# A fused attention and feed-forward kernel: weight splitting spread over six slots, and a tensor operand for a small addition

## Chip, cores, metric

One core of a Trainium2 chip. The metric is the device time of one execution in microseconds (us), the median of several runs; lower is better.

## The reference

```python
def _attn_ref(q, k, v, w1, b1, w2):            # B 4, heads 8, S 576, D 64
    scores = scale * np.matmul(q, k.transpose(0, 1, 3, 2))
    bias = np.maximum(x @ w1 + b1, 0.0) @ w2    # x from positions alone
    scores = scores + bias.transpose(2, 0, 1)[None, :, :, :]
    attn = np.exp(scores - np.max(scores, axis=-1, keepdims=True))
    attn = attn / (np.sum(attn, axis=-1, keepdims=True) + 1e-09)
    return np.matmul(attn, v)
...
x = attn_out.transpose(0, 2, 1, 3).reshape(B * S, H * D)          # 2304 x 512
h = x @ w_in;  x = (h * np.clip(h + 3.0, 0.0, 6.0) / 6.0) @ w_out   # 512 -> 2048 -> 512
x = (sigmoid(x @ w_gate) * (x @ w_val)) @ w_out2                    # 512 -> 1536 -> 512
```

## The kernel before

**Stages.** First the position bias is computed and sent to DRAM (about 0 to 58 us of the span). Then comes the attention (about 57 to 340 us), then the first feed-forward layer (to about 741 us), then the gated one.

**Attention.** The work is 16 attention units n, each two heads of one batch entry; a unit has nine steps s (NSTEP), so there are 144 steps t. The loop at the end of the attention code goes over slots i of two steps each (slot_of_two, L463), so one unit takes four and a half slots and two units take nine. In a slot stand the scores of its two steps (L342, TensorE) with the bias added and the row extreme taken on VectorE (L346), the products with V of an earlier unit (L432, L435, result scaled at L444), the exponentials on ScalarE (L362), and the transposes of the slot before (L400, L408, L415), whose results VectorE and ScalarE copy out of PSUM (L392, L390). After steps 5 and 8 of a unit, invert (L365) adds 1e-9 to the row sums (L368), takes the reciprocal (L369) and spreads it out (L373); turn_inv transposes that one slot later (L379). prep (L304) splits Q and K of the next unit into a high and a low part; its work on GpSimd is at L314 and L318.

**Weights.** The feed-forward weights are split into a high and a low part too. A weight unit is one 128x512 block of 8-byte integers. The Loader makes it in these operations: a DMA of 512 KB into one of two raw buffers (L159), the absolute value of the upper word on ScalarE (L175), a lower bound (the max) on VectorE (L176), a shift on VectorE (L184), two merges with the raw words on VectorE (L186, L188), then the high part on ScalarE and the low part on GpSimd (L192, L193). The first ten units stay in SBUF slots of their own. Before the change, Loader.whole emits a whole unit at once, at slots i = 12, 18, 24, ..., 66 (EVERY is 6). The next units come from Loader.tick, called at slots 70 and 73 (PRIME) and right behind the attention.

**What sets the order.** The program is emitted in the order described, and that order is the priority. A scheduler then lays out each engine's queue at compile time: where its model has an engine free and an operation of lower priority ready, that operation goes ahead. So an operation can stand in its engine's queue earlier than its slot. The DMA of each of the ten units is tied (issue_after) behind the latest load of V on SyncE's queue (L295), which is emitted at step 0 of each attention unit; the other operations of a weight unit are tied to nothing but their data and buffers. Each engine runs its queue in order.

Of the kernel before, what the change touches and what calls it, by code (L numbers as in the profile page):

```python
# [10 lines left out]
F32 = mybir.dt.float32  # L11
F32R = mybir.dt.float32r
I32 = mybir.dt.int32
AF = mybir.ActivationFunctionType
ALU = mybir.AluOpType
# [3 lines left out]
P = 128  # L19
# [6 lines left out]
NSTEP = 9  # L26
# [18 lines left out]


NPRE = 10
EVERY = 6
PRIME = (NU * NSTEP // 2 - 2, NU * NSTEP // 2 + 1)
NALL = 19  # L50

# [45 lines left out]
def block_kernel(ctx: ExitStack, tc: tile.TileContext, q, k, v, mlp, w_in, w_out, w_gate, w_val, w_out2, dist_d,  # L97
                 rows_d, out):
    nc = tc.nc
    pool = lambda **kw: ctx.enter_context(tc.tile_pool(**kw))  # L100
    keep = pool(name="keep", bufs=1)
# [6 lines left out]
    tok = lambda t: [xj[t // 2][:, c, TW * (t % 2) : TW * (t % 2) + TW] for c in range(4)]  # L108
    half = keep.tile([P, 1], F32, name="half")
    one = keep.tile([P, 1], F32, name="one")  # L110
    slots = [keep.tile([P, 2, 512], F32R, name=f"slot{i}") for i in range(NPRE)]
    nbias = [dram.tile([16 * (8 * RK - 1) * (min(P, S - P * c) // 16) + 16], F32, name=f"nbias{c}") for c in range(5)]
    part_d = [dram.tile([P, 4, TW], F32, name=f"part{t}") for t in range(NTILE)]
# [10 lines left out]
    def ring(name):  # L124

        if name == "z":
            return stg.tile([P, 512], F32, name="z", bufs=3)
        return stg.tile([P, 2, 512], F32, name="raw", bufs=2)

    class Loader:  # L130
# [31 lines left out]
        def magnitude(self, i):  # L162
            if i in self.raw:
# [11 lines left out]
                nc.scalar.activation(z, raw[..., 1].bitcast(F32), AF.Abs)  # L175
                nc.vector.tensor_scalar(out=z, in0=z, scalar1=2.0**-15, scalar2=None, op0=ALU.max)  # L176

        def assemble(self, i):
            if i not in self.raw:
                return  # L180
            self.raw.pop(i)
            z, raw = self.z[i]
            zi = z.bitcast(I32)
            nc.vector.tensor_scalar(out=zi, in0=zi, scalar1=3, scalar2=0x3FFFFFF8, op0=ALU.logical_shift_left,  # L184
                                    op1=ALU.bitwise_and)
            nc.vector.scalar_tensor_tensor(out=zi, in0=raw[..., 1], scalar=-0x40000000, in1=zi,  # L186
                                           op0=ALU.bitwise_and, op1=ALU.bitwise_or)
            nc.vector.scalar_tensor_tensor(out=zi, in0=raw[..., 0], scalar=29, in1=zi,  # L188
                                           op0=ALU.logical_shift_right, op1=ALU.bitwise_or)

        def halve(self, z, slot, eng):
            nc.scalar.copy(slot[:, 0], z)  # L192
# [5 lines left out]
        def stage(self, z, idx):  # L198
            hl = self.pair()
            self.halve(z, hl, nc.gpsimd)  # L200
            nc.sync.dma_start(w_d[idx], hl.bitcast(F32))
            self.staged.add(idx)
# [23 lines left out]
                self.mix(to[1], to[2])  # L226
            self.done = i + 1

        def whole(self):
            i = self.n  # L230
            for stage in (self.dma, self.magnitude, self.assemble):
                stage(i)
            self.finish(i, nc.gpsimd)
            self.n += 1

        def tick(self):
            i = self.n
# [24 lines left out]
    load = Loader()  # L262
# [102 lines left out]
    def invert(n, c0, c1):  # L365

        r = sums[n % 3][:, 2 * c0 : min(2 * c1, NSTEP)]
        nc.vector.tensor_scalar(out=r, in0=r, scalar1=1e-9, scalar2=None, op0=ALU.add)  # L368
        nc.vector.reciprocal(r, r)  # L369
        for s0, s1, w in ((0, 6, 64),) if c1 == 3 else ((6, 8, 64), (8, 9, P)):  # L370
            o = spread[:, 64 * s0 : 64 * s0 + (s1 - s0) * w].rearrange("p (s w) -> p s w", w=w)
            i = sums[n % 3][:, s0:s1].unsqueeze(2).to_broadcast(o.shape)
            nc.scalar.copy(o, i)  # L373
# [75 lines left out]
    last_v = [None]  # L449
# [3 lines left out]
    for n in range(NU):  # L453
        i = (NSTEP * n + 5) // 2 + 2
# [8 lines left out]
    def slot_of_two(i):  # L463

        for t in steps(i):
            scores(t)
            n, s = seq[t]
            p, b = divmod(n, B)
            if s == 0:
                last_v[0] = load_v(n)  # L470
            if b == B - 1 and p + 1 < NPAIR and (s % 2 == 1 or s == 8):
                load_bias(p + 1, s // 2)
        for n, a, g in AV.get(i, ()):
            av(n, a, g)
            if g == 4:
                av_out(n, a)
        for t in steps(i):
            expo(t)
        for t in steps(i - 1):
            n, s = seq[t]  # L480
            if s in (5, 8):
                invert(n, s // 6 * 3, s // 6 * 2 + 3)
        for t in steps(i - 2):
            n, s = seq[t]
            if s in (5, 8):
                turn_inv(n, s // 6 * 3, s // 6 * 2 + 3)
        for t in steps(i - 1):
            n, s = seq[t]
            with tc.issue_after(last_s[0].ins):
                trans(t)  # L490
                if s in REM:
                    trans_rem(n, REM[s])
        for t in steps(i):
            if t in PREP:
                n, h = PREP[t]
                prep(n, h)
            for k, (n, h) in PREP.items():
                if h == 1 and n + 1 < NU and t == k + 3:
                    load_qk(n + 1)
# [6 lines left out]
    with ExitStack():  # L506
# [9 lines left out]
        nc.vector.memset(warm, 0.0)  # L516
        nc.vector.memset(half, 0.5)
        nc.vector.memset(one, 1.0)
        nc.scalar.activation(low[0][:, 0:1], one, AF.Relu)
        bias_ps = ExitStack()  # L520
        bp = bias_ps.enter_context(tc.tile_pool(name="bp", bufs=4, space=PSUM))
# [5 lines left out]
        for i in range(2):  # L527
# [5 lines left out]
                                op1=ALU.mult)  # L533
# [30 lines left out]
        for G in range(NG):  # L564
            hid = [hids[(4 * G + ct) % 12] for ct in range(4)]
            nd = max(S - 16 * G, 16 * G + 16)
            for ct in range(4):
# [3 lines left out]
                else:  # L571
                    nc.vector.tensor_scalar(out=hid[ct][:, 0:nd], in0=tbl[:, 0:nd], scalar1=bpsi[:, 1, qd : qd + 1],  # L572
                                            scalar2=None, op0=ALU.max)
# [23 lines left out]
        def split_x(t, cs=range(4)):  # L597
            for c in cs:
                XH, XL = XS[t % 2][:, 0, c], XS[t % 2][:, 1, c]
                nc.scalar.copy(XH, tok(t)[c])  # L600
                eng = nc.gpsimd if 1 in XS else nc.vector
                eng.tensor_tensor(out=XL, in0=tok(t)[c], in1=XH.bitcast(F32), op=ALU.subtract)

        def project(t, slot, ps=None):
            XH, XL = XS[t % 2][:, 0], XS[t % 2][:, 1]
            ps = mp.tile([P, 512], F32, name="h", bufs=4) if ps is None else ps
            for c in range(4):
                wh = slot[:, 0, P * c : P * c + P]
                wl = slot[:, 1, P * c : P * c + P]
                nc.tensor.matmul(ps[:, 0:TW], wh, XH[:, c], start=(c == 0), stop=False)  # L610
                nc.tensor.matmul(ps[:, 0:TW], wl, XH[:, c], start=False, stop=False)  # L611
                nc.tensor.matmul(ps[:, 0:TW], wh, XL[:, c], start=False, stop=(c == 3))  # L612
            return ps[:, 0:TW]

        def hardswish(g, ph):
            nc.scalar.activation(g, ph, AF.Relu, bias=half, scale=1.0 / 6.0)  # L616
            nc.vector.scalar_tensor_tensor(out=g, in0=g, scalar=1.0, in1=ph, op0=ALU.min, op1=ALU.mult)  # L617
            return g
# [5 lines left out]
        for i in range(NSLOT):  # L624
            slot_of_two(i)
            if i == NS // 2:
                w = keep.tile([P, 8 * TW], F32R, name="early")
                XS[0] = w.rearrange("p (r c t) -> p r c t", r=2, c=4)
                split_x(0)
            if i in (NS // 2 + 1, NS // 2 + 2):  # L630
                f = len(begun)
                begun[f] = hardswish(ring("z")[:, 0:TW], project(0, slots[2 * f], pp.tile([P, 2, 512], F32, name="s")[:, 0]))
            if i % EVERY == 0 and i > 10 and load.n < NPRE:
                with tc.issue_after(last_v[0].ins):
                    load.whole()
            if i in PRIME:
                load.tick()

# [185 lines left out]
        def gate_val(base, G, whole):  # L824
            sig, late = {}, {}

            def gate(i, u, ps):
                s = sig[i] = half_t("s", 6)
                if u is None:
                    nc.scalar.activation(s, ps, AF.Sigmoid)  # L830
                else:
                    add(s, u, ps)
                    nc.scalar.activation(s, s, AF.Sigmoid)

            def val(i, u, ps):
                v = ps
                if u is not None:
                    v = half_t("v", 3)
                    add(v, u, ps)
                s = sig[i]  # L840
                last_g[0] = nc.vector.tensor_tensor(out=s, in0=s, in1=v, op=ALU.mult)
                last_h[0] = nc.scalar.copy(G[:, i, 0], s)  # L842
                nc.gpsimd.tensor_tensor(out=G[:, i, 1], in0=s, in1=G[:, i, 0].bitcast(F32), op=ALU.subtract)  # L843

            a, b = Products(base, 0, gate), Products(base, 1, val)
            for p, ks in ((a, range(7)), (b, range(7))) if whole else ((a, range(4)), (b, range(4)), (a, range(4, 7)),
                                                                      (b, range(4, 7))):
                p.run(ks)
# [77 lines left out]
```

## Time and profile before

| what | us |
|---|---|
| median of 3 runs | 1158.08 |
| lowest, highest | 1157.95, 1161.23 |
| the profiled execution | 1160.52 |
| its span | 1158.7 |

TensorE is PE in the profile (PEld is its weight load), VectorE is DVE, ScalarE is ACT, GpSimd is POOL and SyncE is SP. In a timeline row the columns are the start in us from the span's start, the length in us, the engine, the line of the code, the operation, the tiles written and read, and the number of instructions merged into the row. The bracket at the end is idle time of the engine just before, and what ended it. Ends of matmuls are modelled, so distances between starts tell more of PE than its busy time does.

### The profile page before, as it was taken

The page shows a single profiled execution, that of the slowest core. Times are in us where ns is not written, and L with a number is a line of the kernel's source. Part 1 is how long each engine was busy: PE and PEld are TensorE (multiplying, and loading weights), DVE is VectorE, ACT ScalarE, POOL GpSimd, SP SyncE. Part 2 cuts the span into 40 slices and gives each one's busy share as a digit, 9 for nine tenths or more (in the row PEclk, how much of TensorE's full clock was granted, in tenths as well). Part 3 has the DMA queues.
Part 4 walks back from the last instruction along what each step waited for, and adds up shares of the span by engine and source line. Part 5 has one row for each costly group of instructions (what it writes and reads, how often), then busy time and mean ns, then how long its engine had stood idle before and what let it go on. Part 6 is the DMA issues. An engine that isn't in the chain of part 4 may idle for free.

```text
span 1158.7 us, 19146 instructions
## 1 busy us (share of the span) xinstructions
PE 1135.9 (98%) x6862; PEld 1012.2 (87%) x6862; DVE 772.8 (67%) x1495; ACT 588.4 (51%) x1296; POOL 422.6 (36%) x342
## 2 busy tenths in 40 slices
PE   8799999999999999999999999999999999999998
PEld 3277777777779999999999999999899898998997
DVE  8977878788868887355386775585367655644443
ACT  7988887877855545454455454342333222221221
POOL 0154544544316433232347445261333223311211
PEclk9999999999999999999999999999999999999999
DMA  6854436353213665249467759976878848757532
GB/s 203 298 162 110 158 95 183 112 165 103 78 55 110 209 218 200 101 174 340 167 228 255 253 189 357 395 261 251 308 254 309 311 165 299 285 181 258 191 109 73
DMA packets 83183, 236.82 MB, mean 204 GB/s; under 512 B 9616, under 2 KB 12304, under 8 KB 83088
## 3 DMA queue, kind: packets, MB, share of 16 engines
q1 hardware_dynamic: 83088, 235.60, 58.6%
q8 instruction: 54, 0.88, 0.3%
q14 instruction: 41, 0.34, 0.1%
HBM read 154.15 MB, written 81.41 MB: 203 GB/s over the span
## 4 chain that ended last, share of the span: by engine, by line
PE 84%; DVE 6%; ACT 2%; DMA 2%; issue 1%; POOL 1%; SPq 0%; POOLq 0%; DVEq 0%; ACTq 0%
PE o L673 17%; PE h L807 10%; PE o L807 10%; PE s L342 6%; PE o L862 6%; PE h L862 5%; PE h L611 5%; PE h L610 5%; PE h L612 5%; PE av L432 5%; PE tr L400 4%; PE av L435 1%; DVE z L186 1%; DVE u L346 1%; PE tr L379 1%
## 5 line engine op out<-in xcount | busy, mean ns | idle before, releaser
L673 PE MATMUL o<-gh,slot 128*128 128x384 f32 x768 | 196.0, 336 | 1.8 <-DVE take L392 1.8
L673 PEld LDWEIGHTS o<-gh,slot 128*128 128x128 f32 x768 | 139.2, 188 | 2.3 <-DVE take L392 2.1
L673 PE MATMUL o<-gl,slot 128*128 128x384 f32 x384 | 129.1, 336 | 0.7 <-DVE gl L659 0.7
L362 ACT ACTIVATE p<-u,stat 128x576 f32<-128x576 f32 x128 | 98.7, 773 | 29.2 <-DVE stat L346 28.4
L342 PE MATMUL s<-k,q 128*128 128x288 f32 x640 | 111.0, 309 | 0.7 <-ACT ptm L557 0.4
L346 DVE CUSTOM_DVE_ANT_0 u<-s,bias 128x576 f32<-128x576 f32 x128 | 93.6, 753 | 24.4 <-PE s L342 23.2
L843 POOL TENSOR_TENSOR gp<-s,gp 128x384 fp32r<-128x384 f32 x36 | 39.4, 1107 | 177.0 <-ACT gp L842 92.6
L617 DVE SCALAR_TENSOR_TENSOR g<-g,h 128x384 f32<-128x384 f32 x94 | 51.6, 549 | 70.2 <-ACT g L616 70.1
L659 DVE TENSOR_TENSOR gl<-g,gh 128x384 fp32r<-128x384 f32 x94 | 63.1, 671 | 48.3 <-ACT gh L658 45.8
L658 ACT CAST gh<-g 128x384 fp32r<-128x384 f32 x94 | 48.3, 513 | 91.6 <-DVE g L617 91.3
L193 POOL TENSOR_TENSOR hl<-corners,hl 128x512 fp32r<-128x512 f32 x42 | 57.2, 1366 | 94.3 <-ACT hl L192 79.3
L342 PEld LDWEIGHTS s<-k,q 128*128 128x128 f32 x640 | 88.8, 189 | 2.3 <-ACT ptm L557 0.6
L616 ACT ACTIVATE g<-h,half 128x384 f32<-128x384 f32 x94 | 54.3, 578 | 58.4 <-PE h L612 57.9
L807 PE MATMUL o<-x,slot 128*128 128x384 f32 x432 | 78.4, 336 | 1.4 <-DVE sum L787 1.4
L432 PE MATMUL av<-ptm,vn 128*64 128x288 f32 x512 | 77.8, 419 | 0.7 <-DVE x L444 0.7
L807 PE MATMUL h<-x,slot 128*128 128x384 f32 x432 | 77.8, 335 | 0.0
L807 PEld LDWEIGHTS o<-x,slot 128*128 128x128 f32 x432 | 75.1, 188 | 2.0 <-DVE sum L787 1.7
L807 PEld LDWEIGHTS h<-x,slot 128*128 128x128 f32 x432 | 75.2, 188 | 0.7
L400 PE MATMUL tr<-ident,p 128*128 128x128 f32 x512 | 72.2, 275 | 2.2 <-ACT inv L390 1.5
L673 PEld LDWEIGHTS o<-gl,slot 128*128 128x128 f32 x384 | 72.5, 189 | 1.3 <-DVE gl L659 1.3
L314 POOL TENSOR_TENSOR k<-early,one 128x576 fp32r<-128x576 f32 x30 | 34.4, 1167 | 106.3 <-DVE x L572 53.1
L843 POOL TENSOR_TENSOR x<-s,x 128x384 fp32r<-128x384 f32 x36 | 40.3, 1129 | 84.2 <-ACT x L842 50.5
(157 smaller groups left out, 2725.2 us busy)
## 6 DMA issues: line engine op xcount, KB each, us to landing
w<-hl SPq DMA_DIRECT2D x67, 512.0 KB, 3.3
slot<-w SPq DMA_DIRECT2D x67, 512.0 KB, 5.8
raw<-in_part_dram SPq DMA_DIRECT2D x50, 512.0 KB, 4.1
x<-xc SPq DMA_DIRECT2D x56, 384.0 KB, 6.0
sum<-sum SPq DMA_DIRECT2D x72, 256.0 KB, 3.5
early<-xc SPq DMA_DIRECT2D x28, 384.0 KB, 6.4
nbias<-ptm SPq DMA_DIRECT2D x36, 295.5 KB, 3.1
early<-in_part_dram SPq DMA_DIRECT2D x32, 288.0 KB, 4.3
```

Source lines behind the costliest of these rows:

```text
L342: last_s[0] = nc.tensor.matmul(ps[:, a, 0:HS], Q[:, q0 : q0 + P], K[:, r, h, HS * a : HS * a + HS], start=(i == 0), stop=(i == len(mm) - 1))
L346: last_u[0] = nc.vector.tensor_tensor_reduce(out=halves(u), in0=ps[:, :, 0:HS], in1=halves(bt), op0=ALU.add, op1=ALU.min, scale=-0.125, sc ...
L362: nc.scalar.activation(probs(t), us.pop(t), AF.Exp, bias=low[n % 2][:, s : s + 1], scale=-1.0, accum_out=sums[n % 3][:, s : s + 1])
L400: nc.tensor.transpose(ps[:, kc], pts[n, c][:, h, 64 * h + P * kc : 64 * h + P * kc + P], ident)
L432: nc.tensor.matmul(ps[64 * h : 64 * h + 64, 0:HS], vt[:, 4 * h + g], ptm[:, h, g, cols], start=(g == 0), stop=False)
L610: nc.tensor.matmul(ps[:, 0:TW], wh, XH[:, c], start=(c == 0), stop=False)
L611: nc.tensor.matmul(ps[:, 0:TW], wl, XH[:, c], start=False, stop=False)
L659: last_g[0] = nc.vector.tensor_tensor(out=gl, in0=g, in1=gh.bitcast(F32), op=ALU.subtract)
L673: nc.tensor.matmul(os[c][:, 0:TW], sl[:, r, P * c : P * c + P], x, start=(first and r == 0 and x is gh), stop=(last and x is gl))
L807: nc.tensor.matmul(ps[b], sl[:, r, o : o + P], x[:, c, s], start=(k < 4 and i == 0), stop=(i == len(mm) - 1), skip_group_check=True)
L843: nc.gpsimd.tensor_tensor(out=G[:, i, 1], in0=s, in1=G[:, i, 0].bitcast(F32), op=ALU.subtract)
L862: nc.tensor.matmul(os[i], x[:, P * i : P * i + P], slots[(base + 14 + e) % NALL][:, r], start=first, stop=last)
```

## The change

The weight units are no longer emitted whole at every sixth slot. Unit m (0 to 9) starts at slot 9(m+1)//2, which is the slot with step 0 of attention unit m+1, and emits one piece in each of six slots: the DMA; absolute value and max; shift; first merge; second merge; high and low part. So each attention unit from 1 to 10 has one weight unit, and the last piece is emitted in slot 50. Apart from that, the addition of 1e-9 in invert has a tensor operand (one column, broadcast) in place of an immediate.

```diff
-EVERY = 6
...
+    tiny = keep.tile([P, 1], F32, name="tiny")
...
+        def shift(self, i):
+            z = self.z[i][0].bitcast(I32)
+            nc.vector.tensor_scalar(out=z, in0=z, scalar1=3, scalar2=0x3FFFFFF8, op0=ALU.logical_shift_left,
+                                    op1=ALU.bitwise_and)
+
+        def merge(self, i, w):
+            z, raw = self.z[i]
+            z = z.bitcast(I32)
+            scalar, op = ((29, ALU.logical_shift_right), (-0x40000000, ALU.bitwise_and))[w]
+            nc.vector.scalar_tensor_tensor(out=z, in0=raw[..., w], scalar=scalar, in1=z, op0=op, op1=ALU.bitwise_or)
+
         def assemble(self, i):
...
+            self.shift(i)
+            self.merge(i, 1)
+            self.merge(i, 0)
...
-        def whole(self):
-            i = self.n
-            for stage in (self.dma, self.magnitude, self.assemble):
-                stage(i)
-            self.finish(i, nc.gpsimd)
-            self.n += 1
+        def one_step(self, i, k):
+            if k == 0:
+                self.dma(i)
+            elif k == 1:
+                self.magnitude(i)
+                self.raw.pop(i)
+            elif k == 2:
+                self.shift(i)
+            elif k < 5:
+                self.merge(i, 4 - k)
+            else:
+                self.finish(i, nc.gpsimd)
+                self.n = i + 1
...
-        nc.vector.tensor_scalar(out=r, in0=r, scalar1=1e-9, scalar2=None, op0=ALU.add)
+        nc.vector.tensor_tensor(out=r, in0=r, in1=tiny.to_broadcast(r.shape), op=ALU.add)
...
+        nc.vector.memset(tiny, 1e-9)
...
-            if i % EVERY == 0 and i > 10 and load.n < NPRE:
-                with tc.issue_after(last_v[0].ins):
-                    load.whole()
+            for m in range(NPRE):
+                at = i - NSTEP * (m + 1) // 2
+                if 0 <= at <= 5:
+                    with tc.issue_after(last_v[0].ins):
+                        load.one_step(m, at)
```

## Rows read from the trace of the kernel before

**Rows 1.** The page: TensorE, busy us and share of the span.

```profile
PE 1135.9 (98%) x6862; PEld 1012.2 (87%) x6862; DVE 772.8 (67%) x1495; ACT 588.4 (51%) x1296; POOL 422.6 (36%) x342
```

**Rows 2.** Windows: stretch, length; busy us (instructions) of PE, PEld, DVE, ACT, POOL; clock, DMA share, GB/s.

```profile
85.00:119.00 34.00, 34.00 (x255) 26.03 (x254) 25.66 (x71) 27.52 (x73) 17.04 (x14) 1.00 0.46 129
119.00:154.00 35.00, 34.09 (x252) 25.79 (x252) 29.33 (x71) 27.95 (x75) 18.09 (x14) 1.00 0.44 136
...
40.00:50.00 10.00, 6.15 (x60) 1.76 (x60) 9.91 (x27) 9.85 (x21) 0.00 (x0) 1.00 0.92 304
```

**Rows 3.** Timeline of PE: the twelve score matmuls that come once in an attention unit.

```profile
81.86 1.83 PE L342 MATMUL s<-k,q 128*128 128x288 f32 x12
...
100.24 1.83 PE L342 MATMUL s<-k,q 128*128 128x288 f32 x12
...
116.03 1.83 PE L342 MATMUL s<-k,q 128*128 128x288 f32 x12
...
134.71 1.84 PE L342 MATMUL s<-k,q 128*128 128x288 f32 x12
...
151.45 1.84 PE L342 MATMUL s<-k,q 128*128 128x288 f32 x12
...
290.70 1.84 PE L342 MATMUL s<-k,q 128*128 128x288 f32 x12
```

**Rows 4.** Timeline of PE: three stops, and two rows at the same place of two cycles.

```profile
109.76 1.68 PE L432 MATMUL av<-ptm,vn 128*64 128x288 f32 x12
...
128.78 1.68 PE L432 MATMUL av<-ptm,vn 128*64 128x288 f32 x12 [0.22 <-DVE x L444]
...
143.36 0.66 PE L400 MATMUL tr<-ident,p 128*128 128x128 f32 x4 [0.21 <-DVE ptm L392]
...
144.61 1.68 PE L432 MATMUL av<-ptm,vn 128*64 128x288 f32 x12
...
148.48 0.66 PE L400 MATMUL tr<-ident,p 128*128 128x128 f32 x4 [0.48 <-ACT inv L390]
```

**Rows 5.** Instructions on tile z, 60 to 335 us: count, then ns min/median/max.

```profile
L175 ACT ACTIVATE z<-raw x11: 657/682/707, 91.3 to 302.8; 128x512 f32<-128x512 f32 x11
L176 DVE TENSOR_SCALAR z<-z x11: 408/417/1184, 93.5 to 304.4; 128x512 f32<-128x512 f32 x11
L184 DVE TENSOR_SCALAR z<-z x11: 416/428/936, 95.3 to 314.1; 128x512 int32<-128x512 int32 x11
L186 DVE SCALAR_TENSOR_TENSOR z<-raw,z x11: 685/693/1922, 95.7 to 315.8; 128x512 int32<-128x512 int32 x11
```

**Rows 6.** Timeline of DVE and POOL: weight-unit operations, and POOL's work beside them.

```profile
93.53 0.41 DVE L176 TENSOR_SCALAR z<-z 128x512 f32<-128x512 f32 x1
...
124.59 0.42 DVE L176 TENSOR_SCALAR z<-z 128x512 f32<-128x512 f32 x1
...
126.39 1.41 POOL L318 TENSOR_TENSOR q<-early,q 64x576 fp32r<-64x576 f32 x1 [2.22 <-ACT q L310]
...
126.44 1.92 DVE L186 SCALAR_TENSOR_TENSOR z<-raw,z 128x512 int32<-128x512 int32 x1
...
139.39 2.93 POOL L318 TENSOR_TENSOR q<-early,q 64x640 fp32r<-64x640 f32 x2
...
141.43 1.18 DVE L176 TENSOR_SCALAR z<-z 128x512 f32<-128x512 f32 x1
```

**Rows 7.** The addition of 1e-9 and the reciprocal: ns min/median/max, and one row.

```profile
L368 DVE TENSOR_SCALAR stat<-stat x32: 160/168/1149, 65.9 to 328.7; 128x6 f32<-128x6 f32 x16, 128x3 f32<-128x3 f32 x16
...
L369 DVE RECIPROCAL stat<-stat x32: 172/178/195, 66.5 to 328.9; 128x6 f32<-128x6 f32 x16, 128x3 f32<-128x3 f32 x16
...
103.73 1.14 DVE L368 TENSOR_SCALAR stat<-stat 128x3 f32<-128x3 f32 x1 [0.70 <-ACT pm L362]
```

**Rows 8.** Timeline of SP: a load of V and the weight unit's DMA behind it.

```profile
115.32 0.33 SPq L295 DMA_DIRECT2D vn<-in_part_dram  x1
...
116.18 0.42 SPq L159 DMA_DIRECT2D raw<-in_part_dram  x1
```

More of the change, by code (lines that the diff above doesn't have):

```diff
@@ L181, in assemble @@
             self.raw.pop(i)
[L182 to L189, printed above, removed]
+            self.shift(i)
+            self.merge(i, 1)
+            self.merge(i, 0)
         def halve(self, z, slot, eng):
```

## The prediction

> **What bounds the kernel now.** I read the page first: TensorE is busy for 98% of the span [rows 1]. Its busy time is modelled, so I went to the stage that the change touches, the attention, and read the windows. Between 85 and 119 us TensorE has no idle time at all, 34.00 of 34.00 us; between 119 and 154 us 0.91 of 35.00 us is idle [rows 2]. VectorE and ScalarE stay below 30 us in both. So TensorE bounds the attention, and all that an edit of VectorE's or ScalarE's work can return is the time in which TensorE waits for them.
>
> How much is that? The order of the work repeats every two attention units (nine slots), and the twelve score matmuls that come once a unit mark its beat [rows 3]. The first cycle takes 116.03 - 81.86 = 34.17 us, the second 151.45 - 116.03 = 35.42. Two such pairs of cycles are 139.18 us, and 290.70 - 151.45 = 139.25, so the pattern goes on. What differs between the cycles is the weight units: slots 12, 30, 48 and 66 give every other cycle one of them, slots 18 and 24, 36 and 42, 54 and 60 give the cycles between two. Half by half, the long cycle's first half is 18.68 against 18.38 us (+0.30), its second 16.74 against 15.79 (+0.95). Up to the products with V at 144.61 its second half has lost (144.61 - 134.71) - (109.76 - 100.24) = 0.38 us [rows 3, 4], so the other 0.57 goes behind that.
>
> These losses have names. The first stop of TensorE is at 128.78 and waits for the scaling of the attention output; the second at 143.36 waits for a copy out of PSUM; the third at 148.48 waits for a copy on ScalarE [rows 4], late because VectorE is. In front of the first stop stands a merge of the weight unit that took 1.92 us instead of 0.69, beside a GpSimd operation that started at 126.39; in front of the second a max that took 1.18 instead of 0.42 and ended 0.29 us after GpSimd's two operations from 139.39 [rows 5, 6]. The unit of the short cycle (max at 93.53) met no such thing and cost TensorE nothing that can be seen.
>
> **Ceiling of the gain.** Three long cycles lose 0.30 + 0.95 = 1.25 us each: 3.75 us. The medians of this kernel can tell about 0.3%, 3.5 us, from no change. So the whole gain on offer is one such step.
>
> **The spreading, part by part.** The same ten units are made by the same operations: per unit a max and a shift (0.42 us each), two merges of one form (0.69 each), two passes on ScalarE (0.68 by the row of the first), one subtraction on GpSimd and one DMA of 512 KB [rows 5]. Nothing is removed; all of it moves. The terms:
>
> *DMA.* It already goes out 0.9 us behind a load of V [rows 8]. One per attention unit is the same 5 MB in all, on a DMA system at 46% in these windows [rows 2]. On SyncE's queue it stands where it stood in the long cycles. Cost 0; its cover is the slot between landing and use, and without that ScalarE would stand still for the rest of the transfer.
>
> *Units in even attention units (2, 4, 6, 8, 10).* Their max will come where the unit of slot 18 has it (124.59), one slot behind its DMA [rows 6, 8]. What stopped TensorE there was the first merge, at 126.44, in front of the scaling. It is now written two slots later, the shift one slot later. The order of a queue can run ahead of the written order, by a slot or so as the max of slot 12 shows (it ran before slot 12's own work), but then the merge still falls behind the scaling. I take 0 for these five; the upper end is 0.30 each.
>
> *Units in odd attention units (1, 3, 5, 7, 9).* The max is written one slot behind the DMA, and it ran there already (141.43). It will meet the same GpSimd work again, so I keep its 0.38. The shift and the merges, whose delay makes the 0.57, are now in slots of their own behind it: 0. That is 5 x 0.38 = 1.90 us; the ends are 0 and 5 x 0.95 = 4.75.
>
> *The unit of attention unit 1* may run ahead into the bias stage, since the load of V before it isn't held by anything there. VectorE and ScalarE are busy 9.91 and 9.85 of 10 us in that stage [rows 2], so a free place exists hardly before its end. I take 0; the upper end is ScalarE's two passes on the path, 2 x 0.68 = 1.4 us.
>
> *The end of the attention.* Slots 51 to 69 lose their units. Units 10 and up find a free raw buffer sooner and may be made there instead, at the price of the short cycle's unit, 0. What VectorE does behind the last score stays where it is. Cost 0, from -0.3 to +0.3.
>
> **The 1e-9.** 32 additions, median 168 ns but up to 1149 [rows 7]. The long one at 103.73 stands in the short cycle, in which TensorE never stops [rows 2, 7]: what it costs is covered by TensorE's backlog. Would the new form be free of the wait? The reciprocal right behind it, with one input in SBUF, never takes over 195 ns, while the merge with two inputs in SBUF was stretched to 1922 [rows 5, 7]. With the tensor operand the addition has two. So the nearest row is the merge, and the wait stays. Either way the term is 0 us on the path; should the cover go, one late addition costs about 1 us at the next transposes of the row sums. [...]
>
> **The sum.** -3.75 + 5 x 0 + 5 x 0.38 = -1.85 us. The profiled execution took 1160.52 us (span 1158.7, 1.8 around it), 2.4 above the median; it becomes 1158.7. I carry the difference over to the median: 1158.08 - 1.85 = 1156.2 us.
>
> **The rivals.**
>
> *All stops go.* The max, too, falls into a gap of VectorE or of GpSimd. For it: the short cycle's unit, whole and in a row, cost nothing. Against it: nothing moves the max of the odd units. 1158.08 - 3.75 = 1154.3, or 1153.8 with the end of the attention.
>
> *The spreading doesn't happen.* The scheduler may pull the six pieces together again, as its queues run ahead of the written order. Then each even unit costs what slot 18's does and each odd one what slot 24's does: 5 x 0.30 + 5 x 0.95 = 6.25 us in place of 3.75, 1160.6. For it: today's units already stand between other operations, one at a time. Against it: a later place in the program is a lower priority, and VectorE is 75 to 84% busy here.
>
> *Slower: more meetings with GpSimd.* Four operations in four slots meet more of GpSimd's work than four in a row. GpSimd is busy 17.04 of 34.00 us [rows 2]; if the 40 VectorE operations fell beside it by that share, 20 would be blocked. A blocked max cost TensorE 0.38 us for 0.77 of stretch (1.184 - 0.417), so a merge's 1.23 (1.922 - 0.693) would cost 0.61: 10 x 0.38 + 10 x 0.61 = 9.9 us in place of 3.75, 1164.2. It decides from (3.75 + 3.5) / 10 = 0.73 us a unit. For it: three of the eight VectorE operations in the long cycle are stretched, among them a shift (up to 936 ns). Against it: the medians of all four operations are unstretched [rows 5], so it is well under half.
>
> **How the numbers follow.** Forecast 0.45 (its own range 1154.8 to 1157.6), all stops gone 0.25, spreading undone 0.14, slower 0.16. The range reaches from 1153.7 to 1160.9, which takes in the first three and the bounds of the small terms and leaves out the slow case and a little at the lower end. Faster by over 0.3% (under 1154.6) holds nearly all of the second case and a little of the first: 0.27. Slower by over 0.3% (over 1161.6) is the last: 0.16. The rest, 0.57, is within 0.3%.
>
> **What would show it.** Right: the beat of the score matmuls has equal cycles throughout, near 34.2 to 34.6 us; the stops at the scaling (L444) and at ScalarE's copy (L390) are gone; the one at VectorE's copy (L392) comes in each odd attention unit up to 9; from slot 51 TensorE has none; the addition of 1e-9 is still stretched beside GpSimd. Wrong: a stop in even units, more than 10 of 40 operations of the weight units stretched, an attention that starts later than 57 us, or a change of time that arises behind the attention, where I have put nothing.

## The result, and the profile after

| | before | after |
|---|---|---|
| median, us | 1158.53 (1157.95 to 1161.23, 4 runs) | 1167.58 (1167.24 to 1167.88, 4 runs) |
| profiled execution, us | 1160.52 | 1167.37 |
| span, us | 1158.7 | 1165.6 |

The changed kernel takes 1.0073 times as long (95% interval 1.0056 to 1.0091); the medians are 9.05 us apart.

Where is the time? First the beat of the attention, as in [rows 3], from the timeline of PE: the twelve score matmuls that come once in an attention unit. The first row is from before the change, all others are from after it. A half is the time between two of these rows; two halves are one cycle of [rows 3].

```profile
65.49 1.84 PE L342 MATMUL s<-k,q 128*128 128x288 f32 x12
```

```profile
69.02 1.84 PE L355 MATMUL s<-k,q 128*128 128x288 f32 x12
85.09 1.83 PE L355 MATMUL s<-k,q 128*128 128x288 f32 x12
103.55 1.83 PE L355 MATMUL s<-k,q 128*128 128x288 f32 x12
120.33 1.83 PE L355 MATMUL s<-k,q 128*128 128x288 f32 x12
138.73 1.84 PE L355 MATMUL s<-k,q 128*128 128x288 f32 x12
155.49 1.84 PE L355 MATMUL s<-k,q 128*128 128x288 f32 x12
...
260.33 1.83 PE L355 MATMUL s<-k,q 128*128 128x288 f32 x12
278.73 1.83 PE L355 MATMUL s<-k,q 128*128 128x288 f32 x12
294.54 1.83 PE L355 MATMUL s<-k,q 128*128 128x288 f32 x12
312.99 1.84 PE L355 MATMUL s<-k,q 128*128 128x288 f32 x12
```

The first mark was at 65.49 before the change and is now at 69.02: the attention starts 3.5 us late. From there the long halves take 18.46 (85.09 to 103.55) and 18.40, with a weight unit in them, and 18.40 and 18.45 at the end, without one. The short halves take 16.78 and 16.76 with a weight unit and 15.81 (278.73 to 294.54) without: 0.97 us for each odd unit. The stops of TensorE behind that are these. The view lists the waits of PE after, 60 to 335 us: who waited, for whom, us in total, times, longest.

```profile
PE s L355 <- DVE stat L359: 3.0, 1, 3.0
PE tr L413 <- ACT inv L403: 2.0, 4, 0.5
PE tr L413 <- DVE ptm L405: 0.9, 4, 0.2
```

The second line is the third stop of [rows 4] and the third line the second, now four times each, in attention units 3, 5, 7 and 9; the stop at the scaling of the output is gone. The first line is new. The timeline of all engines after, at the start of the attention, shows what stands in front of it:

```profile
13.34 0.44 SPq L159 DMA_DIRECT2D raw<-in_part_dram  x1
...
54.16 3.59 POOL L327 TENSOR_TENSOR k<-early,one 128x576 fp32r<-128x576 f32 x2 [52.73 <-DMA early<-in_part_dram]
...
55.03 0.41 DVE L176 TENSOR_SCALAR z<-z 128x512 f32<-128x512 f32 x1
...
55.48 1.25 DVE L180 TENSOR_SCALAR z<-z 128x512 int32<-128x512 int32 x1
...
56.77 3.46 DVE L187 SCALAR_TENSOR_TENSOR z<-raw,z 128x512 int32<-128x512 int32 x2
...
57.82 1.86 POOL L331 TENSOR_TENSOR q<-early,q 64x640 fp32r<-64x640 f32 x1
...
59.76 3.12 POOL L331 TENSOR_TENSOR k<-early,k 128x576 fp32r<-128x576 f32 x2
60.26 0.76 DVE L359 CUSTOM_DVE_ANT_0 u<-s,bias 128x576 f32<-128x576 f32 x1
...
61.08 2.29 PE L355 MATMUL s<-k,q 128*128 128x288 f32 x8 [3.01 <-DVE stat L359]
```

The first weight unit has run ahead. Its DMA went out at 13.34 us, and its shift and merges (L180, L187) fill VectorE right in front of the first score reduction (L359), each stretched beside GpSimd's split of Q and K: 1.25 + 3.46 us instead of 0.42 + 1.38. The reduction starts at 60.26; before the change it started at 57.76, in this row:

```profile
57.76 0.76 DVE L346 CUSTOM_DVE_ANT_0 u<-s,bias 128x576 f32<-128x576 f32 x1 [2.46 <-PE s L342]
```

TensorE stands still for 3.0 us, and then runs 3.4 us at half clock (granted clock 0.50). These are windows of that stretch after, and of the one half-clock stretch that lay inside the profiled execution before (columns as in [rows 2]):

```profile
60.90:64.30 3.40, 3.22 (x14) 3.20 (x15) 2.37 (x9) 2.50 (x6) 3.32 (x3) 0.50 0.97 334
```

```profile
382.90:386.30 3.40, 3.40 (x12) 3.40 (x12) 3.37 (x6) 1.73 (x4) 1.32 (x1) 0.50 0.98 346
```

Before, the half clock followed a stop of 1.77 us in the first feed-forward layer. That layer took 396.05 us with it (345.53 to 741.58, from the first output product to the first gated one), and 394.57 after, without it.

Second, the gated layer, which the change doesn't name. From its first product to its last it took 413.1 us before and 417.5 after. These are groups of PE there, 780 to 1150 us (busy us, mean ns of one, idle us in front); first before, then after:

```profile
L807 PE MATMUL h<-x,slot 128*128 128x384 f32 x384 | 69.1, 335 | 0.0
L862 PE MATMUL h<-slot,x 128*128 128x512 f32 x146 | 36.2, 391 | 0.0
L807 PE MATMUL h<-early,slot 128*128 128x384 f32 x192 | 36.2, 335 | 0.0
```

```profile
L823 PE MATMUL h<-x,slot 128*128 128x384 f32 x384 | 70.5, 340 | 0.0
L878 PE MATMUL h<-slot,x 128*128 128x512 f32 x144 | 36.3, 395 | 0.0
L823 PE MATMUL h<-early,slot 128*128 128x384 f32 x192 | 36.1, 335 | 0.0
```

The same products on the x tiles, with no stop in front of them, take longer, at granted clock 1.00; those on the tile early don't (335 ns in both). From start to start a product on x takes 176.6 ns instead of 173.3. There are 864 of these products, so they make 2.9 of the 4.4 us; most of the rest is in the products of 512 columns, which are slower too (395 ns against 391 in the rows above).

The balance between the two profiled executions: start of the attention +3.53, the rest of the attention +0.4, first feed-forward layer -1.48 (the half-clock stretch that lay there), gated layer +4.41: +6.9 us, as the spans say. The medians are 9.05 apart: the profiled execution of before, with the half-clock stretch in it, lies 2.0 us above its median, and that of after 0.2 below.

### The profile page after: what moved, and what is told of

Read it like the earlier page. It is cut to its first block, busy times and chain, and to the rows that moved or that the text cites. A ratio compares the mean times of both kernels' runs of the same rounds, so it can differ in the third digit from the quotient of the medians.

```text
span 1165.6 us, 19147 instructions
## 1 busy us (share of the span) xinstructions
PE 1139.6 (98%) x6862; PEld 1014.3 (87%) x6862; DVE 773.9 (66%) x1496; ACT 586.7 (50%) x1296; POOL 427.5 (37%) x342
## 4 chain that ended last, share of the span: by engine, by line
PE 84%; DVE 6%; ACT 2%; issue 2%; POOL 1%; DMA 1%; SPq 0%; DVEq 0%; POOLq 0%; ACTq 0%
PE o L689 17%; PE h L823 10%; PE o L823 10%; PE s L355 6%; PE o L878 6%; PE h L878 6%; PE h L624 5%; PE h L626 5%; PE h L625 5%; PE av L445 5%; PE tr L413 4%; PE av L448 2%; DVE z L187 1%; DVE x L586 1%; PE tr L392 1%
## 5 line engine op out<-in xcount | busy, mean ns | idle before, releaser
L359 DVE CUSTOM_DVE_ANT_0 u<-s,bias 128x576 f32<-128x576 f32 x128 | 93.6, 753 | 23.3 <-PE s L355 22.0
L187 DVE SCALAR_TENSOR_TENSOR z<-raw,z 128x512 int32<-128x512 int32 x76 | 75.9, 1000 | 1.0
```

The lines of the kernel that those rows point to most:

```text
L187: nc.vector.scalar_tensor_tensor(out=z, in0=raw[..., w], scalar=scalar, in1=z, op0=op, op1=ALU.bitwise_or)
L359: last_u[0] = nc.vector.tensor_tensor_reduce(out=halves(u), in0=ps[:, :, 0:HS], in1=halves(bt), op0=ALU.add, op1=ALU.min, scale=-0.125, sc ...
```

## The experiments

Two things are to be told apart: what of it is the spreading and what the small tile, and inside the spreading, why the first unit and the odd ones cost. Ratios are against the kernel before, timed beside each run, with their 95% intervals. A time without an interval is of a single execution; its stages are read from its trace.

**pad32: the tile alone.**

```diff
 one = keep.tile([P, 1], F32, name="one")
+tiny = keep.tile([P, 1], F32, name="tiny")
...
+nc.vector.memset(tiny, 1e-9)
```

> The kernel before with one more column tile (tiny) in the place that the change gives it, filled once and read by nobody; all operations and slots as before. Theory placement: the gated layer loses because every tile behind this one moves by 32 bytes against the x tiles; expected 4 us slower than the kernel before, all of it behind 743 us of the span, with the products on x (L823 after) at about 176 ns from start to start instead of 173, and the attention as before (end within 0.5 us). Rival, the order of the work: the gated layer loses through the moved weight units; expected no change, within 0.5 us.

Measured: 1162.96 against 1158.69 us, 1.0034 (1.0021 to 1.0047). The attention took 288.95 us from the first score matmul to the first output product (288.60 before), the gated layer 417.4, its products on x 176.6 ns. A tile that nobody reads costs 4.3 us, all of it two stages later. The theory of placement came true.

**spread_only: the spreading alone** (the changed kernel with the immediate, without the tile).

```diff
-tiny = keep.tile([P, 1], F32, name="tiny")
...
-nc.vector.tensor_tensor(out=r, in0=r, in1=tiny.to_broadcast(r.shape), op=ALU.add)
+nc.vector.tensor_scalar(out=r, in0=r, scalar1=1e-9, scalar2=None, op0=ALU.add)
```

> The changed kernel without the tensor operand and without its tile: the spreading alone. Theory placement: the gated layer is as fast as before the change, so 4 us below the changed kernel, about 1163.3; the stop ahead of the attention (3 us at 61 us of the span) and the stops in attention units 3, 5, 7 and 9 stay. Rival, the order: 1167, the gated layer slow as in the changed kernel.

Measured: 1163.71 us, 1.0038 (1.0023 to 1.0053); gated layer 413.0, attention 292.4 with the same stops as in the changed kernel. So 5.0 us are the spreading's. With the tile's 4.3 that is 9.3, beside the 9.05 measured for both together.

**tensor_only: the tensor operand alone**, with its value beside the ones.

```diff
-one = keep.tile([P, 1], F32, name="one")
+two = keep.tile([P, 2], F32, name="one")
+one, tiny = two[:, 0:1], two[:, 1:2]
```

> The kernel before with the tensor operand in the addition of 1e-9, its value in the unused room behind the column of ones, so that no tile moves. Theory of the prediction: no change, within 1 us, and additions beside GpSimd stretched as before. Rival, the tensor operand is what makes it slow: 2 us or more slower; rival, the wait goes: additions at 0.2 us throughout, and at most 1 us faster.

Measured: 1158.43 us, 0.9999 (0.9989 to 1.0008). The additions, on the line of tensor_only (ns min/median/max):

```profile
L369 DVE TENSOR_TENSOR stat<-stat,one x32: 152/160/1144, 64.9 to 328.0; 128x6 f32<-128x6 f32 x16, 128x3 f32<-128x3 f32 x16
```

They take as long as the old form did in [rows 7] (1144 ns at most, 1149 there), and within 0.1% it costs nothing.

**pad64, pad_first, pad_behind, pad128: which placement costs.** In all of them the tile is filled and not read: 16 columns; one column in front of the x tiles; one column behind the ten kept slots; 32 columns.

```diff
+tiny = keep.tile([P, 16], F32, name="tiny")   # pad64; pad128: 32 columns
```

```diff
+tiny = keep.tile([P, 1], F32, name="tiny")    # pad_first
 xj = [keep.tile([P, 4, 2 * TW], F32, name=f"x{j}") for j in range(NJ)]
...
 slots = [keep.tile([P, 2, 512], F32R, name=f"slot{i}") for i in range(NPRE)]
+tiny = keep.tile([P, 1], F32, name="tiny")    # pad_behind
```

> The same with a tile of 16 columns, so that everything behind it moves by 64 bytes instead of 32. Theory placement, as a matter of 32 against 64 bytes: no change against the kernel before, within 0.5 us. Rival: any shift of the tiles costs; expected about 4 us slower, as with 32 bytes.

> The kernel before with the unused one-column tile again, but in front of the x tiles, so that the x tiles and all behind them move by the same 32 bytes. Theory distance: what costs is the changed distance between the x tiles and the weight slots; expected no change against the kernel before (within 0.7 us) and 173 ns from start to start in the products on x. Rival, absolute position: the slots stand where they stand with the tile behind the x tiles, so 4 us slower again, with 176 to 177 ns.

> The kernel before with the unused one-column tile behind the ten kept slots: the x tiles and slots 0 to 9 stay, slots 10 to 18 and all the rest move by 32 bytes. Theory distance: only products of x with a moved slot are slower, 9 of 19 slots, so the gated layer takes about 415 us, halfway between 413.1 and 417.4. Rival: the distance of x to another tile, such as the one that holds the other half of the moving data; then 413 or 417.

> The kernel before with an unused tile of 32 columns (128 bytes) behind the x tiles, with all else behind it moved by that. Theory: what counts is the distance of tiles as a remainder of 128 bytes; then the gated layer takes 413 us as before. Rival: any change of the distance costs; 416.5 to 417.5.

| moved against the x tiles | us, or ratio | gated layer, us | products on x, ns |
|---|---|---|---|
| nothing (before) | | 413.1 | 173.3 |
| all, by 32 bytes (pad32) | 1.0034 (1.0021 to 1.0047) | 417.4 | 176.6 |
| all, by 64 (pad64) | 1.0035 (1.0021 to 1.0049) | 416.5 | 176 |
| all, by 128 (pad128) | 1160.71, one execution | 415.1 | 173.3 |
| nothing; x and all moved together by 32 (pad_first) | 1.0005 (0.9995 to 1.0014) | 413.0 | 173.3 |
| slots 10 to 18 and the rest, not slots 0 to 9, by 32 (pad_behind) | 1167.03, one execution | 417.5 | 175.4 |

These are the products on x in the groups of PE, 780 to 1150 us, of pad32 and of pad_first:

```profile
L809 PE MATMUL h<-x,slot 128*128 128x384 f32 x384 | 70.5, 340 | 0.0
L809 PE MATMUL h<-x,slot 128*128 128x384 f32 x384 | 69.1, 335 | 0.0
```

pad_first shows that the place of the slots by itself is not what costs: they stand there as in pad32, but the x tiles moved along, and nothing is lost. In pad64 the rival came true: 64 bytes cost as much as 32. pad128 hit neither of its cases: the products on x are as fast as before, while the gated layer is still 2 us long, mostly in its products of 512 columns (group h<-slot,x: 395 ns, as in the changed kernel). In pad_behind the gated layer lost all of the 4.4 us and not half, as its rival had it, and the first feed-forward layer is slower too (398.7 us, at granted clock 1.00). By slot, in its gated layer, the products on early take 176.8 ns with slots 0 to 9, whose distance to it changed, and 173.6 with slots 10 to 18, whose didn't; that fits the distance. But products on x with slots 0 to 9 took 176.3 ns, and neither of these moved. So the distance between the two operands isn't the whole rule. That another engine's tile, which also moved, takes part in it is a rival that no run tests. The cause stays open.

**aligned_late: without the first unit at the start.**

```diff
-at = i - NSTEP * (m + 1) // 2
+at = i - NSTEP * (m + 2) // 2      # and the tile as in tensor_only
```

> The changed kernel with no tile moved (the small number beside the ones) and every weight unit one attention unit later (2 to 11 instead of 1 to 10). Theory: the stop ahead of the attention comes from the first unit alone, whose shift and merges run ahead of the first score's reduction; without it the first reduction starts near 57.5 us, the half-clock stretch at 61 us is gone, and what stays are stops in the odd units 3 to 11, about 1.0 us each against 3.75 us in the kernel before: about 1160. Rival: the next unit runs ahead in its place, or the start is late for another reason; then 1163.5, as with the spreading alone.

Measured: 1161.29 against 1159.07, 1.0022 (1.0012 to 1.0032), 2.4 us less than the spreading alone. The first reduction starts at 57.42 us, the stop of 3 us and the half clock at 61 us are gone:

```profile
57.42 0.76 DVE L359 CUSTOM_DVE_ANT_0 u<-s,bias 128x576 f32<-128x576 f32 x1 [2.49 <-PE s L355]
```

The odd halves of units 3 to 9 take 16.77 us, that of unit 11 16.47, and the half of unit 12 takes 19.55 instead of 18.4. Operations of the last weight units, the next one pulled ahead among them, stand in and before that half, but TensorE has no stop of 0.15 us in it, so what makes it longer is not shown. Together that is 4 x 0.97 + 0.67 + 1.15 = 5.7 in place of 3.75, so 1.95 us, beside the 2.2 measured.

**tied and tied_late: holding VectorE's operations back.**

```diff
-with tc.issue_after(last_v[0].ins):
+with tc.issue_after(last_v[0].ins), tc.issue_after(last_u[0].ins):
     load.one_step(m, at)
```

> The changed kernel with no tile moved, and with VectorE's operations of a weight unit tied behind the second score reduction of their slot, so that they cannot run ahead of the slot they are written in. Theory: the scheduler undoes the spreading in the odd units, and the first unit hurts because it runs ahead; tied, the start is as in the kernel before, the stops in odd units shrink to the one in front of which the max stands or go: 1154 to 1157. Rival: an operation beside GpSimd's work costs wherever it stands; stops in most of ten units, 1160 or more.

> The same with every weight unit one attention unit later. Theory: as tied, within 0.7 us, since the tie already holds the first unit back. Rival: the first unit costs even when tied, by its DMA or its pass on ScalarE; then this one is 1 us or more faster than tied.

Measured: 1166.49, 1.0066 (1.0049 to 1.0083), and 1169.03, 1.0090 (1.0075 to 1.0105). Both theories fell, and so did the rival of tied_late, which came out slower than tied and not faster. The stop at the start is gone, as expected, and the operations of units 1 to 9 now stand in the slots they are written in. But tied behind the reductions, they stand in front of copies out of PSUM and of additions of 1e-9: TensorE waits five times for a copy (3.1 us in all) and five times for the spread row sums (3.4 us in all), and halves of 16.6 and 19.4 to 20.0 us replace those of 15.8 and 18.4. So even where the spreading holds, it is not free. tied_late had a stop of 2.3 us at 268 us, with the half-clock stretch behind it.

**phases: the odd units further back**, by one, two and three slots.

```diff
-at = i - NSTEP * (m + 2) // 2
+at = i - NSTEP * (m + 2) // 2 - (0, 1, 0, 1, 0, 2, 0, 2, 0, 3)[m]
```

> The changed kernel with no tile moved and the weight units one attention unit later (2 to 11), and those of the odd attention units moved further back: by one slot in units 3 and 5, two in 7 and 9, three in 11. Theory: the odd units cost 0.97 us each because of the place of their max and shift beside GpSimd's work on the next Q and K; a half cycle with such a unit takes 16.77 us now and 15.8 without one, and moved back by two slots or more it falls under 16.2. Rival: the scheduler pulls the operations ahead to the same place, or it is the amount of work in that half; then it stays at 16.7 or more, or the next half takes it over (18.4 grows by as much).

Measured: 1162.41, 1.0024 (1.0013 to 1.0036); every odd half from 3 to 9 still takes 16.76 or 16.77 us. The max of unit 3, in the timelines of VectorE of phases and of aligned_late:

```profile
106.01 1.19 DVE L176 TENSOR_SCALAR z<-z 128x512 f32<-128x512 f32 x1
106.50 1.19 DVE L176 TENSOR_SCALAR z<-z 128x512 f32<-128x512 f32 x1
```

That is 25.18 us behind the mark of its cycle (80.83), and in aligned_late 25.23 (81.27). So the written slot doesn't set the place: the scheduler put the operations where they were. The rival was right in that.

**left_out: one operation less in odd units.**

```diff
-nc.vector.tensor_scalar(out=z, in0=z, scalar1=2.0**-15, scalar2=None, op0=ALU.max)
+if i not in (1, 3):
+    nc.vector.tensor_scalar(out=z, in0=z, scalar1=2.0**-15, scalar2=None, op0=ALU.max)
...
+if i not in (5, 7):
     self.shift(i)
...
+if i != 9:
     self.merge(i, 4 - k)
```

> The changed kernel with no tile moved and the weight units in attention units 2 to 11; of the odd ones, those of 3 and 5 leave out the max, those of 7 and 9 the shift, that of 11 both merges, so the first weights come out without these steps. Which of them makes the 0.97 us of a half cycle (16.77 against 15.8)? Theory: the max and the shift, each stretched beside GpSimd, carry the first of the two stops, and all four by their sum the second: without the max 16.4 or less, without the shift 16.4 or less. Rival: the merges alone, in front of the copies; then 16.7 without max or shift and 15.8 without merges.

Measured, in a single execution of 1161.46 us: 16.55 and 16.54 us without the max, and the same without the shift. That is neither case: each of the two is worth 0.22 us of the 0.97. The half of unit 11, without the merges, took 16.65; in aligned_late it took 16.47 with them, so it says nothing of the merges. Where the max is missing, the shift takes its place and is stretched, and so is the merge behind it, as the timeline of VectorE shows in unit 3:

```profile
105.88 1.20 DVE L181 TENSOR_SCALAR z<-z 128x512 int32<-128x512 int32 x1
107.70 1.20 DVE L188 SCALAR_TENSOR_TENSOR z<-raw,z 128x512 int32<-128x512 int32 x1
```

In aligned_late, with the max in front of them, these two took 0.94 and 0.69 us.

**no_gpsimd: GpSimd's work beside two odd units left out.**

```diff
 high(on[0], Q[0:D], qt)
+if n in (6, 8):
+    return
```

What stands behind this line in prep, and is left out for those two units, is all of GpSimd's part; the line above it is ScalarE's.

> The changed kernel with no tile moved and the weight units in attention units 2 to 11, and with GpSimd's part of the split of Q and K left out for attention units 6 and 8 (they take the stale low and high parts), which is made during units 5 and 7. Theory GpSimd: the stops in odd units come from VectorE's operations waiting beside that split; the half cycles of units 5 and 7 fall from 16.77 to 16.0 us or less, with a max of 0.42 us, while those of 3 and 9 stay at 16.77. Rival, the amount of work: VectorE's 2.2 us too many in that half make the stops; then 5 and 7 stay at 16.5 or more.

The timeline of no_gpsimd: the beat of PE, and VectorE's max in attention units 3 and 5.

```profile
99.66 1.83 PE L357 MATMUL s<-k,q 128*128 128x288 f32 x12
106.37 1.19 DVE L176 TENSOR_SCALAR z<-z 128x512 f32<-128x512 f32 x1
116.42 1.84 PE L357 MATMUL s<-k,q 128*128 128x288 f32 x12
134.80 1.83 PE L357 MATMUL s<-k,q 128*128 128x288 f32 x12
141.52 0.42 DVE L176 TENSOR_SCALAR z<-z 128x512 f32<-128x512 f32 x1
150.51 1.84 PE L357 MATMUL s<-k,q 128*128 128x288 f32 x12
```

With GpSimd's split beside it the half takes 116.42 - 99.66 = 16.76 us and the max 1.19; without it 15.71 and 0.42, with the same four operations on VectorE. Unit 7 shows 15.72, units 3 and 9 keep 16.76 and 16.77. So it is the meeting with GpSimd and not the amount of work. This was a single execution, 1158.95 us; its own units 3 and 9 are what 5 and 7 are compared with.

**even_mix and even_double: the units where they cost nothing**, with no tile moved.

```diff
-at = i - NSTEP * (m + 2) // 2
+at = i - (9, 18, 27, 29, 36, 38, 45, 47, 54, 63)[m]     # even_double
+at = i - (9, 18, 27, 36, 40, 45, 49, 54, 58, 63)[m]     # even_mix
```

> Seven weight units in the even attention units 2 to 14 and three in the odd ones 9, 11 and 13, with no tile moved. Theory: even ones 0, odd ones 0.97 us each, 2.9 us in place of 3.75: about 0.8 us less than the kernel before, 1158. Rival: units 10 and 11, pulled ahead into the last units, cost as they did with units in 2 to 11 (1.1 us): same as before or slower.

> All ten weight units in the halves of even attention units, with no tile moved: starts at slots 9, 18, 27, 36, 45, 54, 63, and three more two slots behind, at 29, 38 and 47. Theory: a unit in an even half costs nothing, and there is room for two: no stops, 3.75 us less than the kernel before, 1155. Rival: the second unit is pulled into the odd half in front or crowds the even one; three halves grow by about 1 us each, 1158.

Measured: even_mix 1158.10 against 1159.27, 0.9990 (0.9981 to 1.0000), with the three odd halves at 16.75 to 16.77 and the halves of units 2 to 8 as without a unit. The interval goes from nothing to 2.2 us; the 0.8 us expected lies in it, but the run can't confirm it. even_double 1156.74, 0.9979 (0.9970 to 0.9988): faster than both kernels. Its beat, in the timeline of PE:

```profile
115.22 1.83 PE L355 MATMUL s<-k,q 128*128 128x288 f32 x12
133.62 1.83 PE L355 MATMUL s<-k,q 128*128 128x288 f32 x12
149.42 1.83 PE L355 MATMUL s<-k,q 128*128 128x288 f32 x12
167.79 1.83 PE L355 MATMUL s<-k,q 128*128 128x288 f32 x12
...
202.24 1.83 PE L355 MATMUL s<-k,q 128*128 128x288 f32 x12
218.33 1.83 PE L355 MATMUL s<-k,q 128*128 128x288 f32 x12
```

The halves are 18.40 and 15.80, 18.37 with two units, and 16.09 where the second unit's last merge falls into the odd half (1.39 us instead of 0.69, in the timeline of VectorE, at 170.55 for the first of the three). The attention of the profiled execution took 285.4 us from its first score matmul to the first output product, 3.2 less than before; the medians say 2.5 us less (1.4 to 3.5 by the interval), of 3.75 on offer.

## Why the prediction was wrong

**The ceiling, borne out.** The prediction held that the cycles differ by the weight units alone, and that 3.75 us is all the attention can give back. even_double, with all its units written in even halves, has no stop left in the waits of PE (60 to 335 us), and took 2.5 to 3.2 us of it. That no arrangement gives more is not shown.

**DMA, even units, the 1e-9: right.** No stop of TensorE in the attention waits for a DMA. The even units cost nothing that can be seen (18.46 and 18.40 with a unit, 18.40 and 18.45 without), and no stop at the scaling is left. With the tensor operand the additions are still stretched beside GpSimd, as predicted (1.14 us at 107.04 in the timeline after, where GpSimd's split of K runs from 106.75 to 108.17), and tensor_only is the same within 0.1%. The reason given was weaker than the result: it chose the merge as the nearest row because both have two inputs in SBUF, but the old addition has one, and took as long (1149 ns at most in [rows 7], 1144 in tensor_only, against 160 and 152 at least). So the rows don't show that the number of inputs matters.

**Odd units: failed.** The step was "The shift and the merges, whose delay makes the 0.57, are now in slots of their own behind it: 0". They aren't. These rows of the timeline after are of attention unit 3:

```profile
108.25 2.94 POOL L331 TENSOR_TENSOR q<-early,q 64x640 fp32r<-64x640 f32 x2
...
110.27 1.19 DVE L176 TENSOR_SCALAR z<-z 128x512 f32<-128x512 f32 x1
...
111.26 1.48 POOL L331 TENSOR_TENSOR k<-early,k 128x576 fp32r<-128x576 f32 x1
...
112.09 0.93 DVE L180 TENSOR_SCALAR z<-z 128x512 int32<-128x512 int32 x1
...
113.31 0.69 DVE L187 SCALAR_TENSOR_TENSOR z<-raw,z 128x512 int32<-128x512 int32 x1
...
116.33 0.68 DVE L187 SCALAR_TENSOR_TENSOR z<-raw,z 128x512 int32<-128x512 int32 x1
```

From the start of the max to that of the last merge it is 6.06 us, as close as slot 24's unit stood before, though written over four slots. The shift ran one slot ahead and both merges two; the max (1.19 us for 0.42) and the shift (0.93 for 0.42) were stretched beside GpSimd. I had the rule (a queue can run ahead "by a slot or so") and took the favourable end of it. That is the rival in which the spreading doesn't happen. In the odd units it was true: 0.97 each, four in the steady part, 3.9 us in place of 3.75, where 1.90 was forecast. In the even units merges ran ahead too, but behind the scaling, and cost nothing. no_gpsimd shows what the 0.97 is: without GpSimd's split beside it, the same four operations cost nothing. And slots of their own are not free either: in tied, where the operations do stand in them, though in another order of the queue, odd halves took 16.6 us and even ones 19.4 to 20.0.

**The first unit: failed, and the argument pointed the wrong way.** "a free place exists hardly before its end", I wrote, took 0, and bounded it by ScalarE at 1.4 us. The free place at the end was the harm: VectorE's last gap before the first score, where GpSimd's split for the first attention unit runs. Shift and merges took 4.7 us there instead of 1.8, and the first reduction came 2.5 us late; with the half clock that follows, the attention starts 3.5 us late. aligned_late, without it, starts like the kernel before.

**The tile: not in the sum at all.** I costed the edit of the addition by its instruction and not by the 32 bytes that it puts between tiles. That is 4.3 us (pad32), nearly half of the result, in the place named under what would be wrong: "a change of time that arises behind the attention, where I have put nothing".

**The sum and the range.** The forecast was a change of -1.85 us, and +9.05 was measured, so 10.9 are to be accounted for: 4.3 for the tile, 3.5 for the first unit, 2.0 for the odd units. No run places the last 1.1 us. The range missed by 6.7 us; it had no room for the tile, and for the first unit 2.1 us too little. The slow rival, more meetings with GpSimd, had the mechanism of the spreading's loss, but not its place: 11 of the 40 operations were stretched, just over the ten named as a sign, three of them in the first unit. One number in the rivals is a slip that changes nothing: with 0.3 us for the end of the attention, all stops gone gives 1154.0 and not 1153.8.

## What to carry to other kernels

Where a scheduler lays out the queues, the written place of an operation off the critical path is a wish: read from the trace how far such operations have run ahead, and what stands free in front of each stage they can reach. In this kernel a VectorE operation was cheap or dear by what GpSimd did beside it (in no_gpsimd the max took 1.19 us with the split beside it and 0.42 without); what helped was to move it to a stretch where GpSimd rests, not merely apart from its like. And a tile that is added moves the tiles behind it: time the allocation alone before judging what the tile is for (here it was 4.3 of 9.05 us).

## What the runs showed of the hardware

The rate of TensorE's products depended on where tiles lie against each other. With everything behind the x tiles moved by 32 or 64 bytes, products on x took 176 to 177 ns from start to start instead of 173.3, at granted clock 1.00 and with no wait in front of them; with x moved along, or all moved by 128 bytes, 173.3. These runs show that TensorE's rate changed with placement alone; what the longer step consists of they don't show.

With the max taken out, which was stretched beside GpSimd (1.19 us in aligned_late), the stretch went to the next operations: the shift behind it took 1.20 us and the merge behind that 1.20 (left_out), against 0.94 and 0.69 with the max in front of them (aligned_late).

The half clock (0.50 for 3.4 us, then 1.00 again) followed a stop of TensorE of 1.8 to 3 us, in the profiled execution of before at 383 us, of after at 61 and of tied_late at 268. Not every such stop had it. These rows, of before and of after, are the same stop in the first feed-forward layer, followed by the half clock in the first and by granted clock 1.00 in the second:

```profile
382.66 0.82 PE L673 MATMUL o<-gh,slot 128*128 128x384 f32 x2 [1.77 <-DVE take L392]
386.56 0.62 PE L689 MATMUL o<-gh,slot 128*128 128x384 f32 x2 [1.77 <-DVE take L405]
```

All seventeen profiled kernels have that stop, of 1.6 to 1.8 us; the half clock followed it in six of them, and the layer then took 395.9 to 396.1 us. Where it didn't, the layer took 394.5 to 395.1 (398.7 in pad_behind, whose products are slower).
